# Operand sums of a Strassen matmul moved from GpSimd to VectorE, their casts moved ahead of another cast, and a second pass that begins where the first one ended

## The chip, the core and the metric

The kernel runs on one core of one Trainium2 chip. Five engines work beside each other, each through its own queue of instructions in order: TensorE (PE, with its weight loads as PEld), VectorE (DVE), ScalarE (ACT), GpSimd (POOL), and SyncE (SP), which here issues nearly all DMAs. Each waits for the others through semaphores. The metric is the time of one execution in microseconds of device time; before the change it was 1484.63 us (median of 3 runs, 1483.06 to 1487.11).

## The reference

Three stages follow one another; the change touches the last one and the end of the second.

```
attn_out = ((q @ k^T) / 8 * decay mask) @ v        # 8 batches x 8 heads, 576 positions of 64
x  = moe(attn_out)                                 # 4608 tokens x 512, 8 experts, top 1, F = 1024
h  = x @ w_in                                      # 4608 x 512 times 512 x 2048
g  = relu(h) ** 2
out = g @ w_out                                    # 2048 x 512
```

All matrix products are made in float32 accuracy by splitting each operand in two float32r parts: `hi` is a cast of the value, `lo` is the value less `hi`, and a product is hi·hi + hi·lo + lo·hi, three matmuls.

## The kernel before

**Three stages.** The attention and the routing run until about 300 us. Then come nine slots of tokens of one expert each (up to 512 tokens, `hpart` and `ypart`), until about 634 us; the last slot is called slot 8 below. From 637 us on runs the dense feed-forward part, called the Strassen stage below: `hquad` (x @ w_in, then relu and square) and `zquad` (g @ w_out).

**The Strassen stage.** It makes two passes over the tokens, since the weights for only half of the 2048 hidden columns fit at a time. In each pass nine groups of 512 tokens are taken in turn (group 8 is made of the early tokens and the last 256), and for each group four *quads* p = 0 to 3, each 512 hidden columns: 72 quads in all, numbered n = 4·s + p with s = 0 to 17. `GSEQ` is the order of the groups, before the change 0 to 8 and again 0 to 8. The results of pass one are written to memory (`zA`), read back in pass two, added, and scattered to the output rows by GpSimd's indirect DMAs (`out<-zo`).

`hquad(n)` makes one step of Strassen's method: instead of eight 256-wide block products, seven products of *sums* of blocks, 42 matmuls. Products 1 and 3 go to the PSUM tile `px`, 4 and 2 to `py`, 5 to `pr_all`, and 7 and 6 on top of what stands in `px`. Between them ScalarE copies the PSUM tiles to the tile `mc` (lines 1334, 1337, 1341), GpSimd adds and subtracts in it (1338, 1339, 1342, 1343), VectorE adds the final `px` (1346) and makes relu and square (1347). ScalarE casts the result to `gh` (1348), and VectorE takes the difference `gl` (1349). There is one tile `mc`, so line 1334 of the next quad has to wait until line 1349 has read it. Products 7 and 6 overwrite `px`, so they have to wait until line 1334 has copied it. `zquad(n-1)`, 24 matmuls of 512 columns, stands behind `hquad(n)` on TensorE.

**The operands.** The seven products of a group need, of x, five sums of two blocks and two plain blocks, each split into hi and lo: `x_fetch` loads the four blocks (`yraw`), `x_prep` has GpSimd make a sum (`xsum`, line 1080), ScalarE cast it (1018) and VectorE take the difference (1019), one after the other. There are two `xsum` buffers. Part 0 makes four of the seven, part 1 the other three; both are called for the following group behind a `zquad`, part 0 in quad p = 1, part 1 in quad p = 2 (one quad later in groups 0 and 9). The weights go the same way (`wq_load`, `wq_prep`, sums at line 1040, two quads at a time through the same `xsum` buffers), and those of the second product without sums (`wo_load`, `wo_split`).

**What sets the order.** The instructions of each engine stand in the order in which the program text calls for them (a manual schedule). For slot 8 the calls are placed by the table `m2` in `OPT`, at numbered ticks, two ticks to each eighth of a slot; `on(t0 + t, ...)` puts them there. In the Strassen stage the `if`s in the last loop decide it. Big tiles come from a pool of 20 buffers, first dropped, first used (`bigt`, `drop`); whoever writes to a buffer waits for its last reader.

Of the kernel before, what the change touches and what calls it, by code (L numbers as in the profile page):

```python
# [123 lines left out]
OPT = dict(manual=True, nbig=10,nlate=10,nx=2,b0=2,bl='SG',rl=2,pz=5,ve=lambda m:'GV' if m<3 or m%4==0 else 'GS',vn=(4,4,2),egn=2,nps=2,npo=1,npt=2,npm=4,nwarm=11,ew=(20,25,32,33),es={23:1,24:1,25:1,26:1,28:1,29:1,30:1,31:1},rlag=1,rlagl=1,rlate=35,rperl=30,e5=5,e6=4,ld=4,rper=8,nw=3,biasat=4,keep=(5,0,4,2),nxw=3,scs=2,e3=13,ylag=2,zlag=2,gb=3,zb=4,cf=(0,6,7,12),cf0=(0,8,9,13),hv=10,zend=1,cwm={0:3},cws={i:(1 if i<4 else 2) for i in range(2,14)},cv0=8,scat=lambda i,n: 2,f3=33,f4=34,f5=34,e0=dict(ro=1,esplit={2:4,3:2,4:2},r1=0,r2=2,r3=2,tab=(7,8,8,9),rec=5,raw=(0,0,1,3),g1=7,split={5:2,6:2,7:2,8:3,9:3,10:2,11:2},xn1=11,tr0=6,tr1=4),hh=3,hl=3,ylag2=1,bs1=dict(regs=1,rec=1,raw=(3,4,5,6),g0=3,g1=7,gn0=(2,)*4,gn1=(2,)*4,split={6:1,7:1,8:2,9:2,10:1,11:2,12:2,13:1,14:2,15:2},tr0=10,tr1=13,cv=1),bs=dict(regs=-9,rec=-9,raw=(0,3,6,8),g0=-4,g1=4,gn0=(1,)*8,gn1=(1,)*8,split={5:1,6:1,7:2,8:2,9:2,10:2,11:2,12:2,13:2},tr0=5,tr1=13,cv=0,f0=7,p0=13,m2={1:('wl',0),2:('xf',),3:('wp',0),5:('xa',),7:('xb',),8:('wl',1),9:('wp',1),10:('ol',0),12:('oh',0),13:('oh',1)}))  # L124


def kernel_body(tc, I, out):
# [873 lines left out]
    GSEQ = [(ph, g) for ph in range(2) for g in range(9)]  # L1001
    tmp = K()
    tmp.n = 0
# [6 lines left out]
    tmp.late = None  # L1010

    def tmp_raw():
        if tmp.late:
            return tmp.late.tile([P, 2, 2, P], F32, name="wraw")
        return B_.cv.tile([P, 4, 2, P], F32, name="wraw", tag="craw")[:, :2]

    def split(hi, lo, x):
        SC.copy(out=hi, in_=x)
        V.tensor_tensor(out=lo, in0=x, in1=hi.bitcast(F32), op=A.subtract)  # L1019

    def wq_load(i):
# [24 lines left out]

    def wo_split(q, h):
        x = slice(2 * h, 2 * h + 2)
        split(*(t[:, x] for t in WO[q]))
        if h:  # L1050
            drop(WO[q][2])

    def x_fetch(n):

        k = XS[n] = K()
        k.raw = bigt("yraw", F32, (P, 4, 512))
        k.mt = sp.tile([P, 4, 2], F32, name="mt", bufs=2)
        hv = HALVES[GSEQ[n][1]]
        for i in range(4):
            kh, j = i // 2, i % 2  # L1060
            y, _, c = hv[j]
            nc.sync.dma_start(out=k.raw[:, i].rearrange("p (a b) -> p a b", a=2), in_=y[:, 2 * kh:2 * kh + 2, c:c + HW])
        for j, (_, mt, c) in enumerate(hv):
            nc.sync.dma_start(out=k.mt[:, 2 * j:2 * j + 2], in_=mt[c:c + HW].rearrange("(j p) w -> p j w", p=P))

    def x_prep(n, part):

        k = XS[n]
        if not part:
            k.ts = [bigt("xq", F32R, (P, 2, 2, 512)) for _ in range(3)]  # L1070
            k.hi, k.lo = ([t[:, j, i] for t in k.ts for j in range(2)] + [xm[:, n % 2, i]] for i in range(2))
            k.ti = sp.tile([P, 4], I32, name="ti", bufs=2)
            V.tensor_copy(out=k.ti, in_=k.mt[:, :, 1])
        b11, b12, b21, b22 = (k.raw[:, i] for i in range(4))
        ops = ((0, b11, b22, A.add), (2, b12, b22, A.subtract), (1, b11, None, None), (3, b21, b11, A.subtract)) if not part else ((6, b21, b22, A.add), (4, b22, None, None), (5, b11, b12, A.add))
        for i, u, v, op in ops:
            x = u
            if op:
                x = tmp_sum()
                G.tensor_tensor(out=x, in0=u, in1=v, op=op)  # L1080
            split(k.hi[i], k.lo[i], x)
        if part:
            drop(k.raw)
# [128 lines left out]
    for s in range(NSURE):  # L1212
        t0 = 8 + 16 * s
        on(t0 + 1, slot_col, s)
        if s + 1 < NSURE:
            b0 = o_.bs1 if s == 0 else bs
            on(t0 + b0["regs"], slot_regs, s + 1)
            on(t0 + b0["rec"], slot_rec, s + 1)
            for n, i in enumerate(WORDER):
                on(t0 + b0["raw"][n], slot_raw, s + 1, i)  # L1220
            for hf in range(2):
                for i, n in enumerate(b0[f"gn{hf}"]):
                    on(t0 + b0[f"g{hf}"] + i, slot_gather, s + 1, hf, n)
# [136 lines left out]
    def zquad(n):  # L1360
# [3 lines left out]
        k = XS[s]  # L1364
# [44 lines left out]

    nq = 4 * len(GSEQ)  # L1410
    for n in range(nq):
        s, p = n // 4, n % 4
        if n == 0:
            wq_load(2)
            wo_load(1)
        hquad(n)
        if n:
            zquad(n - 1)
        if n < 2:
            wq_prep(2 + n)  # L1420
            if n == 0:
                wq_load(3)
            else:
                for h in range(2):
                    wo_split(1, h)
        if s == 8:
            wq_load(4 + p)
        if 33 <= n <= 36:
            wq_prep(n - 29)
        if n in (36, 37):  # L1430
            for h in range(2):
                wo_split(n - 34, h)
        if n in (35, 36):
            wo_load(n - 33)
        if s + 1 < len(GSEQ):
            x = p - (s == 9 or s == 0)
            if x == 0:
                x_fetch(s + 1)
            elif x in (1, 2):
                x_prep(s + 1, x - 1)  # L1440
        if GSEQ[s][0] and p == 1:
            z_back(s)
    zquad(nq - 1)
    esC.close()
# [16 lines left out]
```

## Time and profile before

| what | value |
|---|---|
| median of 3 runs | 1484.63 us (1483.06 to 1487.11) |
| profiled execution | 1487.73 us, span 1485.9 us |
| granted TensorE clock, mean | 0.976 |
| PE busy | 1383.0 us (93%) |
| DVE, POOL, ACT busy | 880.0, 673.7, 520.0 us |
| Strassen stage | 637.6 us to the end |

The span runs from the first instruction to the last; the execution's own time is 1.8 us longer. Every time in a row is counted from the start of the span. Busy times say little here, since matmuls are pipelined and their ends are modelled; the idle time of PE and what ended it say more.

### The profile page before, as it was taken

Reading aid. Unit: us, or ns where it says so; the run is one execution under the profiler, and the core shown is the slowest. Engines: PE = TensorE matmul, PEld = TensorE weight load, DVE = VectorE, ACT = ScalarE, POOL = GpSimd, SP = SyncE. Lnnn points to the kernel's source line nnn. Section 1 sums busy time; section 2 is a strip of 40 time slices with the busy share of each in tenths; the row PEclk is TensorE's granted clock in tenths of the full one; section 3 lists DMA queues with packets and bytes.
Section 4 is the critical chain, followed back from the end, with each engine's and each line's share of the span. In section 5 each row is a group of like instructions: output and inputs, shape, how many; then the busy total and the mean of one; then the engine's idle time right before and its main releaser. Section 6 shows DMA issues by size and latency. Waiting matters only on the chain.

```text
span 1485.9 us, 24925 instructions
## 1 busy us (share of the span) xinstructions
PE 1383.0 (93%) x9728; PEld 1203.5 (81%) x9728; DVE 880.0 (59%) x1259; ACT 520.0 (35%) x992; POOL 673.7 (45%) x765
## 2 busy tenths in 40 slices
PE   9998878999999999979999999998899999999996
PEld 7877678888877778878888888887788888888885
DVE  6667657878776787645545543555654544545442
ACT  3323343444433444433333333333433322333221
POOL 0123354544444433445445443446655654456542
PEclk9999989999999999989999999999999999999998
DMA  8798776656676665331011111012502212122210
GB/s 301 214 219 280 149 179 208 197 179 197 225 227 202 184 208 181 121 109 57 8 51 58 57 57 44 15 57 86 170 32 83 75 68 78 38 85 72 71 54 32
DMA packets 106554, 183.13 MB, mean 123 GB/s; under 512 B 25916, under 2 KB 53436, under 8 KB 101564
## 3 DMA queue, kind: packets, MB, share of 16 engines
q1 hardware_dynamic: 97724, 162.01, 35.8%
q0 software_dynamic: 8704, 19.45, 4.3%
q8 instruction: 78, 1.28, 0.4%
q14 instruction: 48, 0.39, 0.1%
HBM read 134.64 MB, written 46.77 MB: 122 GB/s over the span
## 4 chain that ended last, share of the span: by engine, by line
PE 27%; POOL 9%; DVE 6%; issue 6%; ACT 3%; DMA 2%; SPq 1%; POOLq 0%; DVEq 0%; ACTq 0%
PE zp L1377 5%; PE zp L1378 5%; PE zp L1380 5%; PE px L1324 3%; DVE xq L1019 3%; PE px L1326 3%; PE px L1325 3%; POOL out L1394 2%; DVE mc L1347 2%; POOL xsum L1080 2%; POOL mc L1338 1%; POOL mc L1339 1%; DMA yraw<-yT 1%; POOL mc L1342 1%; PE py L1326 1%
## 5 line engine op out<-in xcount | busy, mean ns | idle before, releaser
L1346 DVE TENSOR_TENSOR mc<-px,mc 128x512 f32<-128x512 f32 x72 | 49.8, 692 | 314.7 <-POOL mc L1342 308.7
L1377 PE MATMUL zp<-woh,gh 128*128 128x512 f32 x576 | 233.2, 405 | 0.0
L1378 PE MATMUL zp<-wol,gh 128*128 128x512 f32 x576 | 232.5, 404 | 0.0
L1338 POOL TENSOR_TENSOR mc<-mc 128x256 f32<-128x256 f32 x72 | 53.7, 746 | 317.1 <-ACT mc L1337 316.9
L1348 ACT CAST gh<-mc 128x1024 fp32r<-128x1024 f32 x72 | 75.5, 1049 | 345.9 <-DVE mc L1347 341.2
L548 POOL DMA_INDIRECT xg<-xl,rix x136 | 137.2, 1009 | 122.1 <-DVE rix L541 78.6
L1080 POOL TENSOR_TENSOR xsum<-yraw 128x512 f32<-128x512 f32 x90 | 153.2, 1719 | 48.5 <-DVE xq L1019 25.2
L1380 PE MATMUL zp<-woh,gl 128*128 128x512 f32 x576 | 165.7, 393 | 0.0
L1349 DVE TENSOR_TENSOR gl<-mc,gh 128x1024 fp32r<-128x1024 f32 x72 | 92.3, 1282 | 84.5 <-ACT gh L1348 84.5
L1378 PEld LDWEIGHTS zp<-wol,gh 128*128 128x128 f32 x576 | 112.4, 195 | 23.5
L1377 PEld LDWEIGHTS zp<-woh,gh 128*128 128x128 f32 x576 | 112.5, 195 | 23.1
L1380 PEld LDWEIGHTS zp<-woh,gl 128*128 128x128 f32 x576 | 108.7, 189 | 25.3
L639 PE MATMUL yp<-hh,whi 128*128 128x512 f32 (+2 forms) x352 | 124.6, 362 | 4.6 <-ACT hh L619 4.2
L1324 PE MATMUL px<-xq,wqh 128*128 128x256 f32 x432 | 124.1, 287 | 3.0 <-DVEq L1292 3.0
L1326 PE MATMUL px<-xq,wql 128*128 128x256 f32 x432 | 124.4, 288 | 0.0
L1325 PE MATMUL px<-xq,wqh 128*128 128x256 f32 x432 | 124.0, 287 | 0.0
L639 PE MATMUL yp<-hh,wlo 128*128 128x512 f32 (+2 forms) x352 | 123.9, 360 | 0.0
L520 DVE TENSOR_TENSOR wlo<-raw,whi 128x512 fp32r<-128x512 f32 x160 | 110.3, 728 | 21.5 <-ACT whi L519 20.8
L1347 DVE SCALAR_TENSOR_TENSOR mc<-mc 128x1024 f32<-128x1024 f32 x72 | 114.1, 1584 | 8.3 <-DVE mc L1346 0.9
L519 ACT CAST whi<-raw 128x512 fp32r<-128x512 f32 x160 | 91.0, 616 | 23.6 <-DMA raw<-in_w 19.1
L614 PE MATMUL hp<-xhi,whi 128*128 128x512 f32 (+1 forms) x256 | 98.9, 386 | 0.0
L615 PE MATMUL hp<-xlo,whi 128*128 128x512 f32 (+1 forms) x256 | 98.9, 386 | 0.0
(226 smaller groups left out, 3364.4 us busy)
## 6 DMA issues: line engine op xcount, KB each, us to landing
raw<-in_w SPq DMA_DIRECT2D x34, 1024.0 KB
kqv<-in_kqv SPq DMA_DIRECT2D x108, 256.0 KB
yraw<-yT SPq DMA_DIRECT2D x68, 256.0 KB
zA<-zo SPq DMA_DIRECT2D x36, 256.0 KB
zo<-zA SPq DMA_DIRECT2D x36, 256.0 KB
xl<-xr SPq DMA_DIRECT2D x34, 256.0 KB
craw<-in_wi SPq DMA_DIRECT2D x16, 512.0 KB
cw<-cm SPq DMA_DIRECT2D x32, 256.0 KB
```

Of the source, the lines that this page charges most:

```text
L520: V.tensor_tensor(out=lo[:, j], in0=raws[i][:, j], in1=hi[:, j].bitcast(F32), op=A.subtract)
L548: G.indirect_dma_start(out=g.x[:, a].rearrange("p k j -> p (k j)"), out_offset=None, in_=xl.rearrange("t (b e) -> (t b) e", b=4)[0:4 * P * ...
L614: PE.matmul(hp, w1h[:, kc, cs], xh[:, kc], start=(kc == 0), stop=False)
L639: PE.matmul(hf.yp[dd], w2[:, fb, dd * P:(dd + 1) * P], h, start=start and f == 0 and (w > HW or dd % 2 == 0), stop=stop and f == 7, skip_g ...
L1080: G.tensor_tensor(out=x, in0=u, in1=v, op=op)
L1324: PE.matmul(o, w[0][:, m, kc], hi[:, kc], start=start and kc == 0, stop=False, skip_group_check=True)
L1325: PE.matmul(o, w[0][:, m, kc], lo[:, kc], start=False, stop=False, skip_group_check=True)
L1326: PE.matmul(o, w[1][:, m, kc], hi[:, kc], start=False, stop=stop and kc == 1, skip_group_check=True)
L1347: V.scalar_tensor_tensor(out=c, in0=c, scalar=0.0, in1=c, op0=A.max, op1=A.mult)
L1377: PE.matmul(zps[s][j], at(gh, j), wh[:, fb], start=(p == 0 and f2 == 0), stop=False)
L1378: PE.matmul(zps[s][j], at(gh, j), wl[:, fb], start=False, stop=False)
L1380: PE.matmul(zps[s][j], at(gl, j), wh[:, fb], start=False, stop=(p == 3 and f2 == 1))
```

## The change

The x sums go from GpSimd to VectorE (`x_sums`) and stand behind a quad's `gl` and differences, one step ahead of their casts. The casts of x and of the weights (`split`) are called in the next quad from a list `gaps`, just ahead of ScalarE's cast of `gh`; the differences (`los`) are kept back and run behind `gl` (`run_los`). The sums of the weights stay on GpSimd, but are written into the weight's own raw tile, a big buffer (`wqr`), and not to `xsum`. Loads stand at the start of a quad (`before`) or behind it (`tails`). The first part of w_out is loaded in quad 0 instead of slot 8. Pass two takes the groups in the order 8, 0, 1, ..., 7 and keeps the x operands of group 8, so that one group is neither loaded nor split again.

```
-m2={1:('wl',0),2:('xf',),3:('wp',0),5:('xa',),7:('xb',),8:('wl',1),9:('wp',1),10:('ol',0),12:('oh',0),13:('oh',1)}
+m2={1:('wl 0','xf'),4:('ws 0','xs 0'),5:('xh 0',),6:('wh 0 0',),7:('xs 1',),8:('xh 1',),9:('wh 0 1','wl 1','xs 2'),10:('xh 2','xp 1'),11:('xp 4','ws 1'),12:('wh 1 0',),13:('wh 1 1',)}
-    GSEQ = [(ph, g) for ph in range(2) for g in range(9)]
+    GSEQ = [(0, g) for g in range(9)] + [(1, g) for g in [8] + list(range(8))]
     def split(hi, lo, x):
         SC.copy(out=hi, in_=x)
-        V.tensor_tensor(out=lo, in0=x, in1=hi.bitcast(F32), op=A.subtract)
+        los.append(lambda: V.tensor_tensor(out=lo, in0=x, in1=hi.bitcast(F32), op=A.subtract))
+        if not tmp.late:
+            run_los()
+    los = []
...
+    XPART = ((0, 2), (3, 6), (5,))
+    def x_sums(n, part):
...
+        for i in XPART[part]:
+            u, v, op = ops[i]
+            k.sum[i] = tmp_sum()
+            V.tensor_tensor(out=k.sum[i], in0=u, in1=v, op=op)
...
         V.scalar_tensor_tensor(out=c, in0=c, scalar=0.0, in1=c, op0=A.max, op1=A.mult)
+        for fn in gap:
+            fn()
         SC.copy(out=gh, in_=c)
         V.tensor_tensor(out=gl, in0=c, in1=gh.bitcast(F32), op=A.subtract)
-        if p == 3:
+        run_los()
+        if p == 3 and s != 8:
             drop(*k.ts)
...
+    at(before, 0, wq_load, 2)
+    at(before, 0, wo_load, 0)
+    at(before, 0, wq_load, 3)
+    at(gaps, 0, wo_splits, 0)
+    at(tails, 0, wq_sums, 2)
+    at(gaps, 1, wq_splits, 2)
+    at(tails, 1, wq_sums, 3)
+    at(tails, 1, wo_load, 1)
+    at(gaps, 2, wq_splits, 3)
+    at(gaps, 2, wo_splits, 1)
+    at(gaps, 2, run_los)
+    for i in range(4):
+        at(tails, 32 + i, wq_load, 4 + i)
+        at(tails, 33 + i, wq_sums, 4 + i)
+        at(gaps, 34 + i, wq_splits, 4 + i)
+    for i in range(2):
+        at(tails, 34 + 2 * i, wo_load, 2 + i)
+        at(gaps, 35 + 2 * i, wo_splits, 2 + i)
+        at(gaps, 35 + 2 * i, run_los)
+    for s in range(len(GSEQ) - 1):
+        if s == 8:
+            continue
+        n, x = 4 * s + (s == 0), s + 1
+        at(before, n, x_fetch, x)
+        at(tails, n, x_meta, x)
+        for i in range(3):
+            at(tails, n + i, x_sums, x, i)
+            d = gaps if n + i + 1 < 4 * x else before
+            at(d, n + i + 1, x_split, x, i)
+            if i < 2:
+                at(gaps, n + i + 1, x_plain, x, (1, 4)[i])
+            else:
+                at(d, n + i + 1, x_done, x)
+        at(tails, n + 1, x_index, x)
+    for s in range(9, 18):
+        at(tails, 4 * s + 1, z_back, s)
     for n in range(nq):
...
+        for fn in before.pop(n, ()):
+            fn()
+        run_los()
+        hquad(n, gaps.pop(n, ()))
         if n:
             zquad(n - 1)
...
+        for fn in tails.pop(n, ()):
+            fn()
```

In the changed kernel the lines of the Strassen stage have other numbers: 1371, 1374 and 1378 are ScalarE's copies, 1375 to 1380 GpSimd's sums in `mc`, 1383 and 1384 VectorE's add and square, 1387 and 1388 `gh` and `gl`; 1012 and 1013 are the cast and the difference of a split, 1092 the x sums.

ScalarE in quads p = 1 and p = 2 of a group of pass one, before: `xq`, `xm` are the hi parts of the next group's operands, `mc` the copies out of PSUM.

```order
L1348 CAST gh<-mc 128x1024
L1018 CAST xq<-xsum 128x512 x2
L1018 CAST xq<-yraw 128x512
L1018 CAST xq<-xsum 128x512
L1334 COPY mc<-px 128x512
```

The same place after the change: first the copies of quad p = 1, then three casts, then `gh`, and then at once the copy that frees `px` in quad p = 2.

```order
L1371 COPY mc<-px 128x512
L1374 COPY mc<-py 128x2x256
L1378 COPY mc_10237<-pr_all 128x256
L1012 CAST xq<-xsum 128x512 x2
L1012 CAST xq<-yraw 128x512
L1387 CAST gh<-mc 128x1024
L1371 COPY mc<-px 128x512
```

What moved: the four casts between `gh` and the next quad's copy of `px` are gone from there; three of them stand ahead of `gh`, one went to a later quad.

VectorE in quads p = 0 to p = 2 of a group of pass one, after the change: `xsum` is the sum that GpSimd made before, `zo` the result of pass one on its way out.

```order
L1383 TENSOR_TENSOR mc<-px,mc 128x512
L1384 SCALAR_TENSOR_TENSOR mc<-mc 128x1024
L1388 TENSOR_TENSOR gl<-mc,gh 128x1024
L1426 TENSOR_SCALAR zo<-zp,mt 128x512 x2
L1092 TENSOR_TENSOR xsum<-yraw 128x512 x2
L1383 TENSOR_TENSOR mc<-px,mc 128x512
L1384 SCALAR_TENSOR_TENSOR mc<-mc 128x1024
L1388 TENSOR_TENSOR gl<-mc,gh 128x1024
L1013 TENSOR_TENSOR xq<-xsum,xq 128x512 x2
L1013 TENSOR_TENSOR xq<-yraw,xq 128x512
L1092 TENSOR_TENSOR xsum<-yraw 128x512 x2
L1081 CAST ti<-mt 128x4
```

What moved: two sums stand behind the results of the group before, a quad ahead of the differences that use them; in the kernel before VectorE had only the differences.

SyncE at the start of slot 8, before: `yraw` are the blocks of x of group 0, `mt` their scales, `meta` a store of slot 7's result, `wraw` and `wql` blocks of w_in.

```order
-L659 DMA meta<-rec 32x16
-L1062 DMA yraw<-yT 128x2x256 x4
-L1064 DMA mt<-meta 128x2x2 x2
-L1028 DMA wraw<-cw 128x2x128 x2
-L1028 DMA wql<-cw 128x2x128
```

The same place after the change: `wqr` and `wqh` are blocks of w_in, `yT` is slot 7's result, whose `meta` follow it.

```order
+L1034 DMA wqr<-cw 128x2x128 x3
+L1034 DMA wqh<-cw 128x2x128
+L1070 DMA yraw<-yT 128x2x256 x4
+L1076 DMA mt<-meta 128x2x2 x2
+L663 REGISTER_ALU
+L663 DMA yT<-yo 512x1x512
```

What moved: the load of group 0's blocks stands ahead of the stores of slot 7's result, not behind them.

## Rows read from the trace of the kernel before

**Rows 1.** Waits of PE: who was waited for, total us, times, longest us.
```profile
PE px L1324 <- ACT mc L1334: 51.5, 22, 5.4
...
PE yp L639 <- ACT hh L619: 4.2, 3, 3.3
```

**Rows 2.** Windows: length, busy us of PE to POOL (instructions), PE clock, DMA.
```profile
637.58:686.63 49.05, 41.53 (x240) 37.85 (x241) 26.44 (x26) 17.86 (x31) 32.37 (x31) 0.90 0.24 74
686.63:1000.16 313.53, 300.45 (x1849) 269.35 (x1848) 157.97 (x158) 108.60 (x178) 142.81 (x147) 0.99 0.15 48
1000.16:1100.68 100.52, 89.99 (x529) 80.02 (x528) 58.35 (x62) 40.03 (x68) 62.30 (x62) 0.95 0.32 105
1100.68:1426.28 325.60, 305.27 (x1849) 272.86 (x1848) 160.86 (x172) 98.29 (x164) 171.70 (x203) 0.97 0.21 65
1426.28:1447.42 21.14, 21.14 (x133) 19.04 (x132) 7.74 (x10) 4.40 (x8) 10.10 (x16) 1.00 0.26 78
```

**Rows 3.** Timeline of ACT, quads 9 and 10: start us, us, instruction [idle before].
```profile
750.09 1.05 ACT L1348 CAST gh<-mc 128x1024 fp32r<-128x1024 f32 x1 [4.53 <-DVE mc L1347]
752.45 0.62 ACT L1018 CAST xq<-xsum 128x512 fp32r<-128x512 f32 x1 [1.31 <-POOL xsum L1080]
...
757.17 0.62 ACT L1018 CAST xq<-xsum 128x512 fp32r<-128x512 f32 x1 [1.36 <-POOL xsum L1080]
757.70 0.58 ACT L1334 COPY mc<-px 128x512 f32<-128x512 f32 x1
```

**Rows 4.** Timeline of SP, then of POOL, in the same stretch.
```profile
743.59 2.14 SPq L1062 DMA_DIRECT2D yraw<-yT  x4
...
751.12 3.52 POOL L1080 TENSOR_TENSOR xsum<-yraw 128x512 f32<-128x512 f32 x2 [2.86 <-DMA yraw<-yT]
```

**Rows 5.** A group of DVE by shape, from 637 us: count, busy us, mean ns, idle.
```profile
L1019 DVE TENSOR_TENSOR xq<-xsum,xq 128x512 fp32r<-128x512 f32 x68 | 48.9, 730 | 4.0 <-ACT xq L1018 1.3
```

**Rows 6.** Timelines of quads 40 to 42: DVE, then POOL, then PE.
```profile
1107.64 1.23 DVE L1347 SCALAR_TENSOR_TENSOR mc<-mc 128x1024 f32<-128x1024 f32 x1
...
1111.46 2.72 DVE L1392 SCALAR_TENSOR_TENSOR zo<-zp,mt,zo 128x512 f32<-128x512 f32 x4
...
1119.94 0.69 DVE L1346 TENSOR_TENSOR mc<-px,mc 128x512 f32<-128x512 f32 x1 [5.77 <-POOL mc L1342]
1120.74 2.19 DVE L1347 SCALAR_TENSOR_TENSOR mc<-mc 128x1024 f32<-128x1024 f32 x1
...
1112.51 1.20 POOL L1394 DMA_INDIRECT out<-zo,ti  x1 [4.96 <-DVE zo L1392]
...
1117.53 0.75 POOL L1338 TENSOR_TENSOR mc<-mc 128x256 f32<-128x256 f32 x1
...
1120.57 3.53 POOL L1080 TENSOR_TENSOR xsum<-yraw 128x512 f32<-128x512 f32 x2
...
1128.92 0.58 PE L1324 MATMUL px<-xm,wqh 128*128 128x256 f32 x1 [3.34 <-ACT mc L1334]
```

**Rows 7.** Timeline of PE in slot 8.
```profile
605.82 0.34 PE L614 MATMUL hp<-xhi,whi 128*128 128x384 f32 x1
...
610.05 0.34 PE L614 MATMUL hp<-xhi,whi 128*128 128x384 f32 x1
...
619.31 0.52 PE L614 MATMUL hp<-xhi,whi 128*128 128x384 f32 x1
```

**Rows 8.** Timelines at the end of slot 8 and in quad 0: ACT, SP, POOL.
```profile
611.39 0.62 ACT L1018 CAST xq<-xsum 128x512 fp32r<-128x512 f32 x1 [7.00 <-POOL xsum L1080]
...
598.38 0.64 SPq L663 DMA_DIRECT2D yT<-yo  x1
...
604.04 1.96 SPq L1062 DMA_DIRECT2D yraw<-yT  x4
...
646.44 0.46 SPq L1045 DMA_DIRECT2D wor<-cw  x1
...
648.28 1.05 ACT L1348 CAST gh<-mc 128x1024 fp32r<-128x1024 f32 x1 [3.68 <-DVE mc L1347]
```

More of the change, by code (lines that the diff above doesn't have):

```diff
@@ L1021, in wq_load, with run_los, drop_later @@
+        if not tmp.late:
+            run_los()
+    los = []
+    def run_los():
+        while los:
+            los.pop(0)()
+    def drop_later(t):
+        los.append(lambda: drop(t))
+        if not tmp.late:
+            run_los()
     def wq_load(i):
-        hi, lo = (bigt(n, F32R, (P, 8, 2, P)) for n in ("wqh", "wql"))
-        raw = tmp_raw()
-        WQ[i] = (hi, lo, raw)
+        k = WQ[i] = K()
+        k.hi, k.lo = (bigt(n, F32R, (P, 8, 2, P)) for n in ("wqh", "wql"))
+        k.raw = bigt("wqr", F32, (P, 8, 2, P))
@@ L1043, in wo_load, with wq_split @@
+    def wq_split(i, part):
+        k, x = WQ[i], slice(4 * part, 4 + 3 * part)
+        split(k.hi[:, x], k.lo[:, x], k.raw[:, x])
+        if part:
+            drop_later(k.raw)
     def wo_load(q):
         WO[q] = hi, lo, raw = bigt("woh", F32R), bigt("wol", F32R), bigt("wor")
-        nc.sync.dma_start(out=raw, in_=cw[4 + q].rearrange("p (a b) -> p a b", a=4))
+        for h in range(2):
+            x = slice(2 * h, 2 * h + 2)
+            nc.sync.dma_start(out=raw[:, x], in_=cw[4 + q].rearrange("p (a b) -> p a b", a=4)[:, x])
@@ L1064, in x_fetch, with x_index @@
             nc.sync.dma_start(out=k.mt[:, 2 * j:2 * j + 2], in_=mt[c:c + HW].rearrange("(j p) w -> p j w", p=P))
-    def x_prep(n, part):
+    def x_index(n):
         k = XS[n]
[L1069 to L1073, printed above, removed]
-        b11, b12, b21, b22 = (k.raw[:, i] for i in range(4))
[L1075 to L1083, printed above, removed]
+        k.ti = sp.tile([P, 4], I32, name="ti", bufs=2)
+        V.tensor_copy(out=k.ti, in_=k.mt[:, :, 1])
@@ L1085, in x_first, with x_split, x_plain, x_done @@
+    def x_split(n, part):
+        for i in XPART[part]:
+            x_one(n, i, XS[n].sum.pop(i))
+    def x_plain(n, i):
+        x_one(n, i, XS[n].raw[:, {1: 0, 4: 3}[i]])
+    def x_done(n):
+        drop_later(XS[n].raw)
     def x_first():
@@ L1309, in kernel_body, with hquad @@
     SLOT = ((0, 2), (3, 1))
-    def hquad(n):
+    def hquad(n, gap):
         s, p = n // 4, n % 4
-        k = XS[s]
+        k = XS[8 if s == 9 else s]
         w = WQ[4 * GSEQ[s][0] + p]
@@ L1410, in kernel_body, with at, wo_splits, wq_splits @@
     nq = 4 * len(GSEQ)
-    for n in range(nq):
[L1412 to L1416, printed above, removed]
+    before, gaps, tails = ({} for _ in range(3))
+    def at(d, n, fn, *a):
+        d.setdefault(n, []).append(lambda: fn(*a))
+    def wo_splits(q):
+        for h in range(2):
+            wo_split(q, h)
+    def wq_splits(i):
+        for h in range(2):
+            wq_split(i, h)
+    at(before, 0, wq_load, 2)
+    at(before, 0, wo_load, 0)
@@ L1417, in kernel_body @@
+    for s in range(9, 18):
+        at(tails, 4 * s + 1, z_back, s)
+    for n in range(nq):
+        for fn in before.pop(n, ()):
+            fn()
+        run_los()
+        hquad(n, gaps.pop(n, ()))
         if n:
             zquad(n - 1)
[L1419 to L1442, printed above, removed]
+        for fn in tails.pop(n, ()):
+            fn()
     zquad(nq - 1)
+    assert not before and not gaps and not tails
```

74 lines of the change are left out of this document (42 added, 32 removed).

## The prediction

> **What bounds the kernel now.** I read the waits of PE first. In the Strassen stage PE waits for one thing alone: 51.5 us in 22 waits, the longest 5.4, before line 1324 for ScalarE's line 1334 [rows 1]. These matmuls are product 7, which overwrites `px` and needs the copy of line 1334. The windows by stage come next, cut where the first matmul of quads 0, 4, 32, 40, 68 starts. Quads 68 and 69 prepare nothing for a later group and show what a quad costs undisturbed: 21.14 us for two, PE busy throughout, clock 1.00 [rows 2], so 10.57. Held against that, quads 4 to 31 (pass one) take 313.53 - 28 x 10.57 = 17.6 us too long, quads 32 to 39 (the change of pass) 100.52 - 84.56 = 16.0, and quads 40 to 67 (pass two) 325.60 - 295.96 = 29.6 [rows 2]. That is more than the waits, because behind one the clock falls from 2.4 to 1.2 GHz for a moment: 0.97 to 0.99 and 0.95 in these windows, not 1.00 [rows 2].
>
> The timeline of ScalarE tells why line 1334 is late. After `gh` at 750.09 ScalarE has casts for the next group in its queue. The first waits 1.31 us for GpSimd's sum, the last 1.36, and only at 757.70 comes the copy that PE waits for [rows 3]. GpSimd itself waited for the load of `yraw` until 751.12, and its two sums then take 3.52 us [rows 4]. ScalarE is not short of time: it was idle for 4.53 us just ahead of that `gh` [rows 3].
>
> **Pass one, -17.0 us.** Each group has five sums of x and seven casts. The sums go to VectorE. The trace has none there, but a subtraction of the same shape with both operands in SBUF: 0.73 us mean [rows 5]. From above the price is bounded by GpSimd's own 1.76 us (3.52 for two [rows 4]). I take 0.73, the same engine and shape. Five are 3.7 us a group; VectorE is busy for 157.97 of 313.53 us in pass one [rows 2], and with 7 x 3.7 = 26 more it is at 59%. They stand behind `gl`, one quad ahead of their casts, so nothing waits for them. The casts of a quad, at most three, cost 3 x 0.62 = 1.9 us and now lie in the 4.53 us that ScalarE idles ahead of `gh` [rows 3]; their inputs are ready a quad earlier. Behind `gh` only line 1334 is left. Without that cover they would push `gh` and `gl` back, and the next quad's line 1334 with them, since there is one `mc`. I leave 0.6 us of the 17.6, because quad 4 begins with a cast ahead of line 1334 (0.62 [rows 3]).
>
> The loads of x come at the start of a group. A load takes from 743.59 to 751.12, 7.5 us [rows 4]. In quad 40 the square ends at 1107.64 + 1.23 = 1108.87, 8.2 us after the quad's start at 1100.68 [rows 2, 6]; `gh` (1.05), `gl` (1.23) and one difference (0.73) more, and the buffer is free 11.3 us into the last quad of a group, 0.7 into the next group. So the blocks lie there 8 us into a group. VectorE asks for them after the four results of 1111.46 to 1114.18 [rows 6], 13.5 us into it (in pass one there are two, so some 12).
>
> **Pass two, -27.6 us.** Here GpSimd also scatters, and that stays. The four scatters begin at 1112.51, so GpSimd's first sum in `mc` starts only at 1117.53 and VectorE's add at 1119.94 [rows 6]. The square then took 2.19 us beside GpSimd's x sums (3.53 us from 1120.57); in the quad before it took 1.23 [rows 6]. With these sums gone: add 1119.94, square 1120.74 to 1121.97, `gh` 1.05 [rows 3] to 1123.1, `gl` (as many columns as the square, taken like it) to 1124.4, line 1334 (0.58 [rows 3]) to 1125.0. Product 7 was ready at 1128.92 - 3.34 = 1125.58 [rows 6]. So the whole wait goes, with 0.5 us to spare; what is late next is this chain itself. For seven groups I leave 2.0 us of the 29.6.
>
> The Trainium skill ("SBUF — State Buffer", section "Who interferes with whom") says that a VectorE instruction with two SBUF inputs and a GpSimd instruction that reads SBUF exclude each other, and whichever starts first holds the port to its end. By that rule the square's 2.19 against 1.23 us is a wait for a GpSimd sum, as here, and the moved sums would do the same to GpSimd.
>
> **Change of pass, -13.5 us.** Group 8 opens pass two with the operands that it has: seven casts, five sums, a load less. The weights of four quads still go through GpSimd and ScalarE, now with a raw tile each, loaded a quad or more ahead. A new wait stands in quads 35 and 37 (and 2): differences of weights ahead of `gl`, two of w_out and two of w_in, 1024, 1024, 1024 and 768 columns. By 1.23 us for 1024 columns [rows 6] that is 4.6 us. After the square, 8.2 us into a quad, `gl` ends at 8.2 + 4.6 + 1.2 = 14.0, and line 1334 at 14.6. Product 7 of the next quad is due at 10.57 + 3.75 = 14.3 (1125.58 less 1100.68 + 2 x 10.57 [rows 2, 6]). So 0.3 us late; where GpSimd's weight sums stretch the square to 2.19 [rows 6], 1.3. With the clock 2.5 us for the two, left of the 16.0. Bounds: 1 and 6.
>
> **Slot 8, -5.0 us.** One eighth of the slot takes 610.05 - 605.82 = 4.23 us, the next 619.31 - 610.05 = 9.26 [rows 7]: 5.0 lost, 3.3 of it a wait for ScalarE's line 619 [rows 1], which stood behind casts that waited 7.00 us for the sums of group 0 [rows 8]. Their blocks were loaded only at 604.04, behind the stores from 598.38 on [rows 8]. Now the load stands ahead of these stores: about 6 us earlier, so casts at 605.4 instead of 611.39, and PE needs line 619 at 612. The loss goes. Bounds: nothing gained, if its buffers are not free earlier, and 5.0.
>
> **Start of pass one, +1.0 us.** The first half of w_out's weights, 1 MB, is now loaded in quad 0, at the place in SyncE's queue where a load of the same size stood before (646.44 [rows 8]). By the 7.5 us of [rows 4] it lands by 654; its casts now stand ahead of quad 0's `gh` (648.28 before [rows 8]), so that `gh` and quad 1 come up to 6 us later. Against that, quad 1 was the longest wait of all (5.4 [rows 1]), and the weight casts that made it leave that place. Bounds: 4 us gained, 6 lost; I take 1.0 lost.
>
> **The sum.** -17.0 - 27.6 - 13.5 - 5.0 + 1.0 = -62.1 us. The profiled execution took 1487.73 us (span 1485.9 and 1.8 around it) and comes to 1425.6; the median of the runs lies 3.1 lower, 1484.63, and comes to 1422.5. I predict 1422.
>
> **Rivals.** (1) The scatter still bounds pass two. Only 0.5 us of spare time stands against it, and if the add comes later than 1119.94, all of the 29.6 us could stay: 1422 + 27.6 = 1450. For it speaks that GpSimd's chain from 1112.51 is not shortened; against it, that the price of the square is read from rows. 6%. (2) The moved sums hold up GpSimd. VectorE's two sums follow its four results of 1111.46 [rows 6], so they run while GpSimd scatters; if each costs GpSimd its 0.73 us, the add comes 1.5 later, 1.0 beyond the spare time, and seven groups pay 7 us, with some clock: 1430. 12%. [...] (3) The edges cost more than they give: the weights land late in quads 0, 2, 35 and 37, at 4 us each: 1438. For it, two loads of 1 MB in these quads; against it, most are issued a quad ahead. 6%. (4) Slower: VectorE's queue is held by the load. The x sums stand ahead of the add of quad p = 1, which comes 10.57 + 6.2 = 16.8 us into a group (the square's 1107.64 less 0.8 [rows 6]); two sums take 1.5, so blocks that land later than 15.3 us into it hold the add, `mc` and PE. I count on 8. To lose the 62 us in 16 groups each must be 3.9 us later than that: loads of 18.5 us instead of 7.5. Beyond that it is slower, at 19.5 us a load some 1500. Nothing in the profile speaks for it; DMA is 15% busy in pass one [rows 2]. 3%. (5) The change does not do what it says (line 1334 waits for something that the rows don't show): about 1484, 2%.
>
> **How the numbers follow.** My forecast has 71%, its own range 1410 to 1432 (start -4 to +6, slot 8 from 0 to -5, the change of pass with 1 to 6 us left). Rival 2 lies inside, rival 3 mostly above. From 1408 to 1442 no more than 2 in 10 is left out: rivals 1, 4, 5 and the half of 3. All losses named come to 68 us, and with a start that gains 4 the floor is near 1412, a little lower if the clock stays up. A measurement can tell 0.3% (4.5 us) from no change. Faster: forecast, rivals 1 to 3, 95%; same 2%; slower 3%.
>
> **What would show it.** Right: PE's wait for line 1371 (1334 before) falls from 51.5 us to under 10; the quads of both passes take 10.6 us; VectorE's square is 1.23 us nearly throughout; no wait for line 619 in slot 8. Wrong: ScalarE's `gh` starts later in quads p = 1 and 2 because a cast ahead of it waits for a sum; VectorE waits for `yraw`; pass two keeps waits of 2.8 us in quads p = 2.

## The result, and the profile after

The changed kernel takes 1431.11 us (median of 4 runs, 1423.62 to 1433.62), the kernel before 1485.87 beside it: a ratio of 0.962, 95% interval 0.958 to 0.967. I had predicted 1422, range 1408 to 1442. All ratios here leave out one execution, of the kernel with every x sum made twice, which took 3154.02 us. The profiled execution took 1433.08 us (span 1431.3): 54.65 less than before, where the sum said 62.1.

Waits of PE after the change (who was waited for, total us, times, longest us), to be held against [rows 1]:

```profile
PE px L1361 <- ACT mc L1371: 18.1, 4, 10.2
...
PE px L1363 <- DVE wql L1013: 1.2, 1, 1.2
PE yp L639 <- ACT hh L619: 1.1, 1, 1.1
```

The wait for ScalarE's copy (1334, now 1371) fell from 51.5 us in 22 waits to 18.1 in four; the prediction wanted less than 10. The wait for line 619 that is left lies at 485 us, in an earlier slot; slot 8 has none. The windows, cut at the starts of quads 0, 4, 32, 40, 68 and 70 as in [rows 2], show where the four waits lie:

```profile
634.30:686.53 52.23, 40.69 (x240) 36.94 (x241) 26.16 (x27) 19.89 (x30) 23.99 (x26) 0.87 0.36 110
686.53:983.57 297.04, 295.53 (x1849) 266.13 (x1848) 152.06 (x195) 108.07 (x177) 81.55 (x112) 1.00 0.15 47
983.57:1077.09 93.52, 86.35 (x529) 77.48 (x528) 55.76 (x55) 37.41 (x55) 50.71 (x52) 0.98 0.32 102
1077.09:1371.86 294.77, 294.77 (x1849) 265.80 (x1848) 169.03 (x204) 99.35 (x161) 119.57 (x168) 1.00 0.23 72
1371.86:1392.93 21.07, 21.07 (x133) 19.00 (x132) 8.38 (x11) 4.32 (x8) 10.09 (x16) 1.00 0.25 80
```

In pass two (fourth row) PE is busy for the whole window at clock 1.00; in pass one (second row) it lacks 1.5 us, all in quad 4 (one of the four waits, 0.66 us, and 0.85 for a difference of VectorE's). The other three waits stand in the first and third rows, where the granted clock is 0.87 and 0.98. In pass one ScalarE's row of work now reads so (quads 9 and 10, as in [rows 3]):

```profile
745.31 1.14 ACT L1012 CAST xq<-xsum 128x512 fp32r<-128x512 f32 x2
746.36 0.62 ACT L1012 CAST xq<-yraw 128x512 fp32r<-128x512 f32 x1
749.56 1.05 ACT L1387 CAST gh<-mc 128x1024 fp32r<-128x1024 f32 x1 [2.59 <-DVE mc L1384]
753.44 0.59 ACT L1371 COPY mc<-px 128x512 f32<-128x512 f32 x1 [2.82 <-PE px L1363]
```

Here no cast waits for a sum, and the copy waits for PE, no longer PE for the copy. In pass two (quads 41 and 42, VectorE, GpSimd, ScalarE, PE, as in [rows 6]):

```profile
1090.23 1.28 DVE L1092 TENSOR_TENSOR xsum<-yraw 128x512 f32<-128x512 f32 x2
1096.09 0.69 DVE L1383 TENSOR_TENSOR mc<-px,mc 128x512 f32<-128x512 f32 x1 [4.57 <-POOL mc L1379]
1096.89 1.23 DVE L1384 SCALAR_TENSOR_TENSOR mc<-mc 128x1024 f32<-128x1024 f32 x1
1099.29 1.23 DVE L1388 TENSOR_TENSOR gl<-mc,gh 128x1024 fp32r<-128x1024 f32 x1 [1.17 <-ACT gh L1387]
...
1102.24 2.39 DVE L1092 TENSOR_TENSOR xsum<-yraw 128x512 f32<-128x512 f32 x2
```

```profile
1090.15 0.97 POOL L1434 DMA_INDIRECT out<-zo,ti  x1 [0.17 <-issue]
...
1093.68 0.74 POOL L1375 TENSOR_TENSOR mc<-mc 128x256 f32<-128x256 f32 x1
...
1101.91 1.01 POOL L1375 TENSOR_TENSOR mc<-mc 128x256 f32<-128x256 f32 x1 [5.16 <-ACT mc L1374]
```

```profile
1100.61 0.59 ACT L1371 COPY mc<-px 128x512 f32<-128x512 f32 x1 [1.35 <-DVE gl L1388]
```

```profile
1101.70 0.28 PE L1361 MATMUL px<-xm,wqh 128*128 128x256 f32 x1
```

The square takes 1.23 us instead of 2.19. The copy ends at 1101.20, 0.50 before product 7 starts at 1101.70 without a wait: the prediction said 0.5. In slot 8 the eighths take 4.24 and 4.21 us, where one took 9.26 [rows 7]:

```profile
608.00 0.34 PE L614 MATMUL hp<-xhi,whi 128*128 128x384 f32 x1
...
612.24 0.34 PE L614 MATMUL hp<-xhi,whi 128*128 128x384 f32 x1
...
616.45 0.34 PE L614 MATMUL hp<-xhi,whi 128*128 128x384 f32 x1
```

The remaining waits, in quads 1 (10.24 us), 36 (2.67) and 38 (4.51), follow ScalarE's casts of w_out. ScalarE after quads 0, 35 and 37:

```profile
649.31 1.04 ACT L1012 CAST woh<-wor 128x1024 fp32r<-128x1024 f32 x1 [9.18 <-DMA wor<-cw]
650.92 1.05 ACT L1012 CAST woh<-wor 128x1024 fp32r<-128x1024 f32 x1 [0.56 <-DMA wor<-cw]
651.87 1.04 ACT L1387 CAST gh<-mc 128x1024 fp32r<-128x1024 f32 x1
...
1025.45 2.25 ACT L1012 CAST woh<-wor 128x1024 fp32r<-128x1024 f32 x2 [4.47 <-DMA wor<-cw]
1027.61 1.04 ACT L1387 CAST gh<-mc 128x1024 fp32r<-128x1024 f32 x1
...
1050.90 1.05 ACT L1012 CAST woh<-wor 128x1024 fp32r<-128x1024 f32 x1 [5.87 <-DMA wor<-cw]
```

Each time `gh` stands behind a cast that waits for its load, while its own input is ready (the square ends at 1023.79 and 1048.17 in quads 35 and 37). SyncE issues these loads (`wor`) late: the one of quad 35 behind loads of w_in, the one of quad 37 behind the stores of `zA`:

```profile
1018.85 1.38 SPq L1034 DMA_DIRECT2D wqr<-cw  x3
...
1020.85 0.89 SPq L1053 DMA_DIRECT2D wor<-cw  x2
...
1039.28 5.71 SPq L1429 DMA_DIRECT2D zA<-zo  x4
1045.08 1.08 SPq L1053 DMA_DIRECT2D wor<-cw  x2
```

### The profile page after: what moved, and what is told of

It reads as the page before. It is cut to its first block, busy times and chain, and to the rows that moved or that the text cites. A ratio compares the mean times of both kernels' runs of the same rounds, so it can differ in the third digit from the quotient of the medians.

```text
span 1431.3 us, 24859 instructions
## 1 busy us (share of the span) xinstructions
PE 1361.8 (95%) x9728; PEld 1191.1 (83%) x9728; DVE 876.4 (61%) x1320; ACT 517.6 (36%) x969; POOL 534.4 (37%) x675
## 3 DMA queue, kind: packets, MB, share of 16 engines
q8 instruction: 78, 1.28, 0.4%
## 4 chain that ended last, share of the span: by engine, by line
PE 48%; issue 2%; DVE 1%; DMA 1%; ACT 1%; POOL 1%; SPq 0%; POOLq 0%; ACTq 0%; DVEq 0%
PE zp L1420 8%; PE zp L1418 8%; PE zp L1417 8%; PE px L1361 4%; PE px L1363 4%; PE px L1362 4%; PE py L1362 2%; PE py L1363 2%; PE py L1361 2%; PE pr_all L1361 1%; PE pr_all L1363 1%; PE pr_all L1362 1%; DMA wor<-cw 1%; DVE gl L1388 0%; DMA zo<-zA 0%
## 5 line engine op out<-in xcount | busy, mean ns | idle before, releaser
L1417 PE MATMUL zp<-woh,gh 128*128 128x512 f32 x576 | 226.7, 394 | 0.0
L1418 PE MATMUL zp<-wol,gh 128*128 128x512 f32 x576 | 226.6, 393 | 0.0
L1375 POOL TENSOR_TENSOR mc<-mc 128x256 f32<-128x256 f32 x72 | 58.1, 808 | 441.7 <-ACT mc L1374 391.9
L1388 DVE TENSOR_TENSOR gl<-mc,gh 128x1024 fp32r<-128x1024 f32 x72 | 88.8, 1233 | 90.1 <-ACT gh L1387 90.1
L1417 PEld LDWEIGHTS zp<-woh,gh 128*128 128x128 f32 x576 | 108.9, 189 | 21.8
L1418 PEld LDWEIGHTS zp<-wol,gh 128*128 128x128 f32 x576 | 108.7, 189 | 21.6
L1361 PE MATMUL px<-xq,wqh 128*128 128x256 f32 x432 | 122.3, 283 | 3.1 <-DVEq L1329 3.1
L1362 PE MATMUL px<-xq,wqh 128*128 128x256 f32 x432 | 122.7, 284 | 0.0
L520 DVE TENSOR_TENSOR wlo<-raw,whi 128x512 fp32r<-128x512 f32 x160 | 109.9, 727 | 15.7 <-ACT whi L519 15.1
L1371 ACT COPY mc<-px 128x512 f32<-128x512 f32 x72 | 42.3, 587 | 167.2 <-PE px L1363 143.2
L616 PE MATMUL hp<-xhi,wlo 128*128 128x512 f32 (+1 forms) x256 | 98.7, 385 | 0.0
```

Source lines behind the costliest of these rows:

```text
L520: V.tensor_tensor(out=lo[:, j], in0=raws[i][:, j], in1=hi[:, j].bitcast(F32), op=A.subtract)
L616: PE.matmul(hp, w1l[:, kc, cs], xh[:, kc], start=False, stop=(kc == 3))
L1361: PE.matmul(o, w.hi[:, m, kc], hi[:, kc], start=start and kc == 0, stop=False, skip_group_check=True)
L1362: PE.matmul(o, w.hi[:, m, kc], lo[:, kc], start=False, stop=False, skip_group_check=True)
L1417: PE.matmul(zps[s][j], at(gh, j), wh[:, fb], start=(p == 0 and f2 == 0), stop=False)
L1418: PE.matmul(zps[s][j], at(gh, j), wl[:, fb], start=False, stop=False)
```

## Experiments

Theory A: the sums made a quad ahead free pass one, GpSimd freed of them gives the rest of pass two, and the edges lose to w_out's late load. Ratios are to the kernel before on the same chip. The stretches, in us, are cut from each kernel's one trace at the same quads as above.

| kernel | ratio, 95% interval | quads 0-3 | 4-31 | 32-39 | 40-67 |
|---|---|---|---|---|---|
| before | 1 | 49.05 | 313.53 | 100.52 | 325.60 |
| changed | 0.962 (0.958-0.967) | 52.23 | 297.04 | 93.52 | 294.77 |
| before, sums on VectorE | 1.030 (1.027-1.033) | 51.21 | 326.42 | 103.48 | 345.20 |
| before, new group order | 0.996 (0.994-0.997) | 48.32 | 310.55 | 91.66 | 324.99 |
| changed, sums on GpSimd | 0.975 (0.973-0.977) | 52.32 | 299.11 | 92.36 | 310.48 |
| changed, casts behind | 0.958 (0.957-0.960) | 49.89 | 297.51 | 89.10 | 294.77 |
| changed, both of these | 0.976 (0.973-0.978) | 50.42 | 299.39 | 91.75 | 311.55 |
| changed, sums twice | 0.964 (0.963-0.966) | 52.65 | 299.17 | 93.04 | 295.53 |
| changed, late load of x | 0.965 (0.962-0.967) | 52.58 | 297.15 | 93.08 | 294.85 |
| early w_out | 0.958 (0.956-0.960) | 48.00 | 296.91 | 88.32 | 294.99 |
| differences behind gl, quad 35 | 0.963, one run | 52.36 | 297.01 | 94.11 | 294.77 |
| early w_out and that | 0.959 (0.956-0.961) | 46.31 | 297.07 | 90.51 | 294.99 |
| early w_out, casts behind | 0.960 (0.958-0.962) | 48.77 | 297.53 | 90.38 | 294.99 |
| early w_out, x later | 0.954 (0.952-0.957) | 47.00 | 297.06 | 84.21 | 296.33 |

**One part alone: the sums on VectorE, in the old order.**

```
-                G.tensor_tensor(out=x, in0=u, in1=v, op=op)
+                (V if n else G).tensor_tensor(out=x, in0=u, in1=v, op=op)
```

> The kernel before, with one part of the change alone: the x sums of the Strassen stage on VectorE, at the old place right ahead of each cast, casts behind gh. Theory A (pass one needs the quad ahead, pass two only a relieved GpSimd): in pass one VectorE makes sum and difference in turn, and line 1334 comes as late as before, 313 us; in pass two the square is back to 1.23 us and much of the 29.6 us goes: 1460 to 1480 us. Rival E (the engine is all): 1440 to 1450 us.

It is slower by 3%, and both readings missed both passes: pass one takes 326.42 us, pass two 19.6 more than before. VectorE's queue in quad 41:

```profile
1137.38 1.23 DVE L1349 TENSOR_TENSOR gl<-mc,gh 128x1024 fp32r<-128x1024 f32 x1 [1.17 <-ACT gh L1348]
...
1138.59 0.68 DVE L1080 TENSOR_TENSOR xsum<-yraw 128x512 f32<-128x512 f32 x1
1139.96 0.69 DVE L1019 TENSOR_TENSOR xq<-xsum,xq 128x512 fp32r<-128x512 f32 x1 [0.69 <-ACT xq L1018]
1140.57 0.68 DVE L1080 TENSOR_TENSOR xsum<-yraw 128x512 f32<-128x512 f32 x1
```

Sum, cast and difference now take turns, 2 us each, and begin only behind `gl`; GpSimd, with a queue of its own, could start its sums before (at 1120.57 beside the square [rows 6]). PE's wait in these quads grew from 2.85 to 4.69 us, although the square was 1.23. In the old order the faster engine is a loss.

**The two parts undone in the changed kernel, one by one and together.** `G` for `V` in `x_sums` (Strassen stage only); the loop over `gap` behind `gh` and `gl`; both.

```
-            V.tensor_tensor(out=k.sum[i], in0=u, in1=v, op=op)
+            (G if n else V).tensor_tensor(out=k.sum[i], in0=u, in1=v, op=op)
```

> Changed kernel, but the x sums of the Strassen stage go back to GpSimd, still one quad ahead of their casts, which stay ahead of gh. Theory A (GpSimd's chain is what bounded pass two, the order what bounded pass one): in pass one the sums only stretch the square from 1.23 to about 2.2 us, inside 2.4 us of spare time, so pass one stays at 297 us; in pass two 3.5 us of sums stand between the four scatters and GpSimd's sums in mc, the add comes 3.5 us later, 2.9 beyond the spare time, in 8 groups with clock 25 to 30 us: 1455 to 1462 us. Rival C (making the sums a quad ahead is all): 1431 us. Rival E (the engine is all, in both passes): 1475 us.

> Changed kernel, but the casts of x and weights stand behind gh and gl again and not ahead of gh; the sums stay on VectorE and one quad ahead. Theory A (the sums made a quad ahead are what counts): three casts take 1.9 us, 1.2 of it beside gl, so line 1371 comes 0.7 us later, against 2.4 us of spare time in pass one and 0.6 in quads p = 1 of pass two; both passes stay at 10.5 to 10.6 us a quad, the edges gain up to 5 us because gh no longer waits for w_out: 1425 to 1433 us. Rival C (the place of the casts is what counts): most of the 16.5 and 30.8 us of the passes comes back, 1465 us or more.

> Changed kernel with x sums on GpSimd and casts behind gh, but the sums still a quad ahead of the casts. Theory A: pass one near 297 to 300 us, since the sums are still early (2.2 for the square and 0.7 for the casts use up the 2.4 us of spare time), pass two as with sums on GpSimd alone, plus 0.7 us a group: 1460 to 1470 us. If engine and place of the casts were what counted, and not the quad ahead, the old 1485 us.

Pass one stays within 2.4 us of 297 in all four combinations: neither the engine nor the place of the casts frees it. What they share is the sum made a quad ahead; with it come a load of x that starts a quad earlier (in the kernel before the sums waited 2.86 us for it [rows 4]) and sums made in three parts instead of two. No run shows these apart. In pass two the engine counts, 15.7 us with the casts ahead and 16.8 behind, less than the 25 to 30 expected: the two sums take 2.54 us there and not 3.5, and seven groups pay, not eight (GpSimd, then PE's wait):

```profile
1087.14 0.96 POOL L1434 DMA_INDIRECT out<-zo,ti  x1 [0.19 <-issue]
1088.12 2.54 POOL L1092 TENSOR_TENSOR xsum<-yraw 128x512 f32<-128x512 f32 x2
1090.62 0.73 POOL L1375 TENSOR_TENSOR mc<-mc 128x256 f32<-128x256 f32 x1
```

```profile
1098.18 0.39 PE L1361 MATMUL px<-xm,wqh 128*128 128x256 f32 x1 [1.86 <-ACT mc L1371]
```

The place ahead of `gh` gives the passes nothing (0.5 and 0.0 us) and costs 6.8 at the edges (52.23 + 93.52 less 49.89 + 89.10). With the sums on GpSimd it gives them 0.3 and 1.1 us and costs 2.5 at the edges. In the medians neither is resolved, as the intervals overlap.

**One part alone: the new order of groups, in the kernel before** (`GSEQ` as in the change, group 8's operands kept).

> The kernel before, with one part of the change alone: pass two begins with group 8, whose x operands are kept. Theory A: quads 32 to 39 no longer load, sum and cast x of group 0 beside the weights; of their 16.0 us about half goes, the passes stay as they were: 1476 to 1480 us. Rival: the weights alone make those quads late, 1484 us.

1475.19 us against 1482.8. The loss of quads 32 to 39 falls by 8.9 us, a little over half of the 16.0, and the waits in quads 1, 37 and 42 to 66 stay. The whole change gains 7.0 there, so that what it does besides the new order loses some 2 us in these quads.

**Every x sum made twice.**

```
+            if n:
+                V.tensor_tensor(out=k.sum[i], in0=u, in1=v, op=op)
```

> Changed kernel, with each x sum of the Strassen stage made twice on VectorE (80 more instructions of 0.65 us, 52 us of work). Theory A (VectorE has the time, and its sums hold up nobody): the second sum lies behind gl where VectorE is idle; quads stay at 10.5 us, 1431 us within 3. Rival D (VectorE is near its limit in quads p = 1 and 2 of pass two, or its sums hold up GpSimd's scatters and sums in mc): each doubled pair delays the add by up to 1.3 us in pass two, 8 groups with two such quads, +8 to +20 us.

VectorE works 32 us longer in each pass; they take 2.1 and 0.8 us more, the 2.1 all in quad 4. Rival D, which wanted 8 to 20, falls.

**The load of x later in slot 8** (`xf` one tick later, behind the stores).

> Changed kernel, but in slot 8 the load of the first x blocks stands one tick later, behind the stores of slot 7 on SyncE's queue, as before. Theory A (the eighth of 9.26 us came from this load): ScalarE's casts wait again, one eighth of the slot takes 7 to 9 us and the Strassen stage begins 3 to 5 us later: 1434 to 1436 us. Rival: the sums' engine or the place of the casts removed that wait, and the eighths stay at 4.2 us: 1431 us.

```profile
604.35 1.97 SPq L1070 DMA_DIRECT2D yraw<-yT  x4
```

```profile
610.51 1.29 DVE L1092 TENSOR_TENSOR xsum<-yraw 128x512 f32<-128x512 f32 x2 [9.27 <-DMA yraw<-yT]
```

```profile
612.33 0.97 PE L639 MATMUL yp<-hl,whi 128*128 128x384 f32 x4 [2.33 <-DVE hl L620]
```

From the second eighth of slot 8 to quad 0 it takes 38.97 us against 34.76 in the changed kernel (40.23 before). So 4.2 of the 5.5 us won here hang on the load's place on SyncE's queue (one eighth takes 6.82, the next 5.76); where the other 1.3 come from no run shows. The way is another than in the kernel before: there PE waited for ScalarE's line 619, here for VectorE's `hl`, which stands behind the sums that wait for the load. The medians alone (1434.49 and 1431.11) could not tell it.

**w_out loaded earlier.** The raw tile is taken and loaded apart from the other two, the first one in slot 8 behind `ws 1`.

```
-    at(before, 0, wo_load, 0)
...
-        at(tails, 34 + 2 * i, wo_load, 2 + i)
+        if not i:
+            at(tails, 33, wo_load, 2)
...
+        if n == 36:
+            at(before, 36, wo_load, 3)
```

> Changed kernel, but the raw halves of w_out are loaded earlier: the first at the end of slot 8, the second in quad 33, the third in quad 36 ahead of the load of x. Casts and differences stay where they are. Theory A (what is left at the edges is ScalarE's casts of w_out that wait for their load ahead of gh): the waits of 10.2, 2.7 and 4.5 us in quads 1, 36 and 38 go, and with the clock behind them quads 1, 36, 38 lose 12.2 + 3.0 + 6.3 = 21.5 us; ratio to the kernel before 0.9623 - 21.5/1485.9 = 0.948, about 1409 us. Rival B (the weight differences ahead of gl, or the raw buffers that come free late, take the place of the load): at least half of the waits stays, 1420 us or more.

Half right. Quad 1 waits 2.83 instead of 10.24 us and quad 38 0.87 instead of 4.51, but quad 36 waits 2.71 as before, and quad 2 now 3.50 for VectorE's differences of w_in's weights. GpSimd begins the sums for these only when their load has landed, at 641.38 behind the branch after slot 8, and ends them at 647.94; how much of the 3.50 the load makes no run shows. VectorE in quad 35:

```profile
1014.76 1.66 DVE L1386 SCALAR_TENSOR_TENSOR mc<-mc 128x1024 f32<-128x1024 f32 x1
1016.34 3.17 DVE L1013 TENSOR_TENSOR wql<-wqr,wqh 128x1024 fp32r<-128x1024 f32 x2
1019.44 3.43 DVE L1013 TENSOR_TENSOR wol<-wor,woh 128x1024 fp32r<-128x1024 f32 x2
1022.79 1.21 DVE L1390 TENSOR_TENSOR gl<-mc,gh 128x1024 fp32r<-128x1024 f32 x1
```

The four differences ahead of `gl` take 6.5 us (1016.34 to 1022.79), beside GpSimd's weight sums, and hold it even when the load is early.

**These differences behind gl, without and with the early load** (these two and the next kernel ran on a chip where the kernel before takes 1466.74 us).

```
-        at(gaps, 35 + 2 * i, run_los)
+        if i:
+            at(gaps, 37, run_los)
```

> The changed kernel with that one edit alone: in quad 35 the four differences behind gl, w_out loaded as late as in the changed kernel. Theory A: gh still waits for the casts of w_out (1027.61 in the changed kernel's trace), gl follows at once, line 1371 at about 1030.1 instead of 1031.5: the wait of quad 36 falls from 2.67 to about 1.3 us, not to nothing. If the load did not matter at all, it goes to nothing.

> w_out's raw halves loaded early, and in quad 35 alone VectorE's four differences of weights behind gl instead of ahead of it. The early load alone left quad 36's wait at 2.71 us, with 3.17 + 3.43 us of differences between square and gl. Theory A (these differences are a second cause of that wait, each enough by itself): gl ends at 11 us into quad 35 instead of 16.2, line 1371 comes 5 us earlier, the wait of quad 36 goes and the quad takes 10.5 to 10.8 us instead of 13.5; 3 us less than with the early load alone. Rival (GpSimd's weight sums hold the copy's successors back): a wait of 1 us or more stays.

Quad 36 waits 2.67 us with neither repair, 2.71 with the early load, 0.93 with the differences moved, and not at all with both: two causes side by side. The differences alone make the whole wait, the load alone 0.93 us of it. But the ratio did not move (0.959 against 0.958 with the early load alone), since quad 38 now waits 3.42 instead of 0.87. VectorE in quad 37, ahead of the add:

```profile
1015.01 1.82 DVE L1094 TENSOR_TENSOR xsum<-yraw 128x512 f32<-128x512 f32 x2 [1.64 <-DMA yraw<-yT]
1016.76 0.68 DVE L1385 TENSOR_TENSOR mc<-px,mc 128x512 f32<-128x512 f32 x1
```

**Both repairs by way of the casts behind.**

> Both repairs together: w_out's raw halves loaded early, and all casts of the Strassen stage behind gh and gl (with them the weight differences). Theory A: passes as with the casts behind alone, 297.5 and 294.8 us; quads 36 and 38 without a wait, quads 32 to 39 in 85 us; quad 1 without its wait for w_out, a wait for the third weights of w_in stays in quad 2, quads 0 to 3 in 45 to 47 us: 1412 to 1418 us, ratio 0.951 to 0.955, faster than the changed kernel and than either repair. Rival (the two repairs remove the same time): 1422 us.

The rival was nearer in the total (0.960 is no better than either repair alone), but not in its reason: quad 36 has no wait, and quad 38 has one of 4.01 us. ScalarE behind quad 37's `gh`:

```profile
1024.39 1.05 ACT L1387 CAST gh<-mc 128x1024 fp32r<-128x1024 f32 x1 [7.37 <-DVE mc L1386]
1025.34 1.79 ACT L1012 CAST wqh<-wqr 128x1024 fp32r<-128x1024 f32 x2
...
1030.48 0.58 ACT L1373 COPY mc<-px 128x512 f32<-128x512 f32 x1
```

Seven casts, 5.1 us of them, now stand between `gh` and the copy, which could have begun when `gl` ended, at 1026.70. Here the place of the casts does count, and behind is the wrong one.

**The x operands of the next group a quad later.**

```
-        n, x = 4 * s + (s == 0), s + 1
+        n, x = 4 * s + (s in (0, 9)), s + 1
```

In quad 37, too, the differences of weights stand behind `gl`.

> The early load of w_out, the differences of weights behind gl in quads 35 and 37, and besides the load, sums, casts and differences of the x operands of the second group of pass two one quad later (as at the start of pass one). With the wait of quad 36 cured, quad 38 waited 3.42 us, because VectorE's x sums waited 1.64 us for the load of yraw in front of the add of quad 37. Theory A (that load is now the next cause): the x sums come ten us later, find their blocks, no wait is left in quads 36 to 39, quads 32 to 39 take 84.5 to 86 us; quad 40 begins with a cast and a difference ahead of its own work, as quad 4 does, and takes some 12.5 us: 3 to 5 us less than before this edit, ratio 0.955 to 0.957. Rival (GpSimd's weight sums or the chain through mc hold these quads too): quads 32 to 39 stay at 88 us or more.

The windows of quads 32 to 39 and 40 to 67:

```profile
973.07:1057.28 84.21, 84.21 (x529) 75.89 (x528) 52.34 (x49) 37.28 (x54) 53.39 (x52) 1.00 0.36 113
1057.28:1353.61 296.33, 295.46 (x1849) 266.32 (x1848) 172.71 (x208) 100.01 (x163) 119.28 (x168) 1.00 0.23 72
```

The change of pass has no wait left; quad 40 takes 1.4 us more. At 1417.00 us (1484.94 before on this chip; ratio 0.954, the changed kernel's 0.962) it beats both kernels. Two things changed at once in quad 37, though. Of the 3.42 us that quad 38 had waited, the load made at most 1.64; the differences ahead of `gl`, 4.4 us there (1018.68 to 1023.05), went in the same edit, and no run moves one without the other.

## Why the prediction was right or wrong

The time lies in the range, 9 us above the forecast. Both passes and slot 8 came out near the forecast or better; the change of pass lies outside its own bounds, and 3.2 us more from pass two made up for part of it.

**Pass one, -17.0: -16.5.** Right in size, with a sum of 0.64 us (1.28 for two) where I took 0.73. The reason was given too broadly: the sums made a quad ahead do it (with their earlier load). On GpSimd, and with the casts behind `gh`, it is as good within 2.4 us. I expected VectorE to be busy for 26 us more, 59% of the pass; it was busy for 152.06 us, less than the old 157.97, since its squares and differences are no longer stretched.

**Pass two, -27.6: -30.8.** Right in size. The chain came out as computed. I left 2.0 us; nothing is left, and a quad takes 10.53, not 10.57. But I gave it all to the engine, and with the sums a quad ahead the engine is about half (15.7); the other (325.60 to 310.48) came with the sums still on GpSimd, and the engine alone, in the old order, lost 19.6.

**Slot 8, -5.0: -5.5**, 4.2 of it by the load, as argued.

**Start of pass one, +1.0: +3.2,** inside its bounds. The load landed by 651, sooner than my 654. But `gh` came at 651.87, and quad 1 waited 10.24 us, twice the old 5.3; I had set the loss of `gh` against a gain that was not there in full. With the load early some 3 us stay: quad 0 has no `zquad` and takes 6.6 us, and its `gl` comes later than that.

**Change of pass, -13.5: -7.0.** This step failed: 9.3 us (93.52 less 8 x 10.53) were left where I allowed 2.5, bounds 1 and 6. Two things in it were wrong. "Loaded a quad or more ahead" does not hold for w_out: SyncE issues its loads at 1020.85, behind weight loads that wait until 1018.85, and at 1045.08, behind the stores of `zA`, and ScalarE waits 4.47 and 5.87 us for them in front of `gh`. And the differences ahead of `gl`, 4.6 us by 1.23 for 1024 columns, took up to 6.5, as those of 1024 columns take up to 1.76 us beside GpSimd's weight sums. For quad 36 the runs with one and with both repaired show the two apart.

**The sum.** These five differ from the forecast by 0.5 - 3.2 - 0.5 + 2.2 + 6.5 = 5.5 us; 2.2 more is slot 8 that began later in this execution (its second eighth at 599.54, before 597.35), and 0.2 less the last four quads. That is the distance from -62.1 to -54.6. The prediction's own range, 1410 to 1432, does not come out of its bounds, which add up to 1416 to 1436.

**The rivals.** (3), late weights at the edges, came true in three of its quads. (1) and (5) did not. (2), the moved sums holding up GpSimd, came at a seventh of its price where I feared it: beside the scatters the two sums took 1.28 us (at 1090.23), 0.64 each, and from the first scatter to the first sum in `mc` GpSimd took 5.0 us in every group, where six of seven groups had taken 4.8; I had reckoned with 1.5 more. It came again a quad later, beside GpSimd's sums in `mc`: one of these took 1.01 instead of 0.74, and the pair of x sums 2.39 instead of 1.28. The rule of the Trainium skill ("SBUF — State Buffer", section "Who interferes with whom"), by which two such instructions exclude each other, agrees with this trace. But it falls in quad p = 2, whose chain has time; even with the sums doubled pass two took only 0.8 us more. (4), VectorE's queue held by the load of x ahead of an add, happened in quad 37 alone (1.64 and 0.97 us in two kernels), and only when the wait in front of it was cured; with the load late in slot 8 the queue was held there.

## What to carry to other kernels

Prepare an operand a step ahead first, and choose its engine second: in pass one the engine then made no difference, in pass two, where GpSimd also scattered, 15.7 us. The same sum on the faster engine, placed right ahead of its use in a queue that also makes the next step, cost 3%. What is placed ahead of a critical cast must have its load already landed, so count from when the load can be issued, behind all that waits in its queue, not from where the call stands. When two waits lie side by side, curing one may show little or no gain (2.67 us became 2.71 or 0.93); cure both before judging either, and see what waits next.

## What the runs showed of the hardware

A subtraction of 1024 columns on VectorE took 1.23 us alone and up to 1.76 beside GpSimd's sums; a GpSimd sum of 256 columns 0.74 alone and up to 1.77 beside VectorE. A VectorE sum of 512 columns took 0.64 alone and beside GpSimd's scatters, and 1.2 beside GpSimd's sums. One chip ran everything ahead of the Strassen stage faster (quad 0 at 611 to 614 us in three kernels, elsewhere at 627 to 638), but pass one in the same 297.0 to 297.5 us; differences of a few us between kernels are therefore read from stretches, not from medians.
